# Padded strided cells, alternating value cells and a new issue plan in a banded-attention, SoLU and bilinear kernel

## Chip, cores and metric

One core of a Trainium2 chip. The metric is device microseconds of one execution; lower is better. Three runs of the kernel before gave 739.69, 740.57 and 744.24 us.

## What is computed

Three layers follow one another on 2304 tokens (4 batches of 576): causal attention with 8 heads of 64, then a SoLU layer with a layer norm, then a bilinear layer. In attention, heads 0 to 3 see the last 32 keys, and heads 4 to 7 see only the earlier keys whose position has the same remainder modulo 32.

```python
rel = pos[:, None] - pos[None, :]
mask_local = (rel >= 0) & (rel < stride)                                      # heads 0..3, stride 32
mask_strided = (rel >= 0) & (pos[None, :] % stride == pos[:, None] % stride)  # heads 4..7
attn = softmax(where(mask, q @ k.T / 8, -1e9)); x = attn @ v                  # (2304, 512)
h = x @ w_in; solu = h * softmax(h)                                           # w_in (512, 1024)
ln = (solu - mean) / sqrt(var + 1e-6) * g_ln; y = ln @ w_out                  # w_out (1024, 512)
return ((y @ w_a) * (y @ w_b)) @ w_out2                                       # d_ff = 1536
```

## The kernel before

All work is recorded first as a list of operations with an engine, an estimated duration, what they read and write, and a key. A planner (class `Plan`) then issues them: `forward` simulates the five engines, taking at each step the ready operation with the smallest key; `backward` sets new keys from a pass in reverse; 120 rounds with random noise on the keys (from `PARAM["seed"]`) are tried and the plan that its own replay finds shortest is kept. The duration passed to `pe(...)` is thus only a plan's cost, but it decides the order on every engine: TensorE, VectorE, ScalarE, GpSimd, and SyncE's queue of DMA issues. Engines run their instructions in the order issued and wait on semaphores.

**Attention.** Heads go in pairs ("groups"), four per batch: two strided, two local. `group_T` transposes q and k (L624) into `qkT`; for strided groups the evacuation (L632) sorts the positions by remainder, so that each of the 32 remainders is a run of 18 consecutive columns. A head's 16 runs of one parity (`RP`) are taken three at a time: 54 queries against the same 54 keys, a "cell", with the part between different runs masked off. Since 16 = 5 x 3 + 1, the sixth cell has one run: 18 queries and 18 keys (`RUNS`). `att_tile(g, j, ...)` handles one tile: a strided tile is two heads and one parity, 12 cells, two of them with 18 rows; a local tile is up to four blocks of 64 queries with 96 keys, for two heads, 8 cells. There are 16 strided and 24 local tiles in all, in four batches.

In a tile `scores` (L706, L709) writes the mask into a PSUM tile `s` with one full-size bf16 matmul per bank, then adds q k' of each cell. The cell's first operand is loaded as weights (its queries are the columns of the weight tile, 54 or 18 of them), its second moves (its keys). Upper and lower PSUM halves (`half`) alternate between cells; in a strided tile both heads read the partitions of one parity. fp32 operands take two passes, each with a record. Softmax follows on VectorE (maximum, subtraction, sum, reciprocal), ScalarE (exponential) and GpSimd (division, L784; in batch 0 L769 to L781 after it). The probabilities are transposed: in batch 0 in fp32 through TensorE (L769, "direct"), in the others as two fp16 parts by a DMA transpose (L793). `pv` multiplies with the values into `xbank`: in batch 0 one fp32 matmul per cell (L803), in the others three fp16 ones (L808 to L810). Here the values are the weight tile (keys are its rows, 64 value dimensions its columns), and the queries move. The rows of a strided cell start at partition 64 x head and the result lands at partition 64 x head. Then ScalarE writes the result to `xT` (L830).

**The layers behind.** `moe1` makes h with 24 matmuls per 128 tokens (L861), interleaved by the planner with attention; `s2` makes y (L910). Then comes the bilinear layer, matmuls M (L1288) and o (L1353), in three passes over w_a, w_b and w_out2, with fp16 weights split into two parts by ScalarE and VectorE (L1123 and others). Weights arrive in 64-bit form and are rebuilt by `from_f64` (L468 to L481). Of w_in and w_out this happens during the first 100 us.

The order of the cells in a strided tile and the plan's cost of the score operation:

```python
cells = [... for p in reversed(range(NG)) for h in range(2) for half in range(2)
         for r in (2 * p + half,) if r < len(RUNS) ...]
pe(ng * nk * 0.42e-3 + sum(0.04 if c[3] else 4 * c[7] / 2.4e3 for c in cells) + 0.03, scores, ...)
```

So the cells with the short run come second and fourth: head 0 with 54 rows, head 0 with 18, head 1 with 54, head 1 with 18, and then eight with 54.

Of the kernel before, what the change touches and what calls it, by code (L numbers as in the profile page):

```python
# [48 lines left out]
PSCALE = 4096.0  # L49
LSCALE = 1024.0  # L50
NEG = -(2.0 ** 120)
PASSES = ((0, 0), (0, 1), (1, 0))

PARAM = dict(back=12, first=40, early=(0,), seed=4, noise=0.1, direct=(0,), span=4.0, dense=1500, cols=5000, pf1=(),
             pf2=(), ph1=(), pv=(), pp=(8,), ps1=(), ps2=(), passes=120, e=3,
             PT=3, raw=2, rawl=2, raws=2, qkT=2, V=2, wk=2, xt=1, ln=2, lnT=2, ys=2, raw64=3, f64f=4, att=100.0,
             win=24.5, wout=128.6, moff=-69.7, moe=96.6, conv2=257.2, dconv=15.0, p2=385.0, pre=6.5, fine=(),
# [38 lines left out]
class Plan:  # L96
# [43 lines left out]
    def latency(self, a, b):  # L140
        if a.eng == b.eng and a.eng != "SP":
            return self.SAME[a.eng]
        return PARAM["lat"] * (0.28 if a.eng == "PE" else 0.14)

    def schedule(self):
# [4 lines left out]
        best, keys = self.length(order), [o.key for o in self.ops]  # L150
        rnd = random.Random(PARAM["seed"])
        for n in range(PARAM["passes"]):
            if n % PARAM["back"] == 0 and n >= PARAM["first"]:
                for o, key in zip(self.ops, keys):
# [4 lines left out]
            for o in self.ops:  # L159
                o.key += rnd.gauss(0.0, PARAM["noise"]) - o.sooner  # L160
            self.shift = self.TICK * (n % 4) / 4
# [73 lines left out]
    def forward(self):  # L235
# [13 lines left out]
        for _ in self.ops:  # L249
# [4 lines left out]
            if e == "PE":  # L254

                while recent and recent[0][0] < at - PARAM["span"]:
                    recent.popleft()
# [29 lines left out]
def tile_banded_attention_solu_bilinear(  # L287
# [13 lines left out]
    nc = tc.nc  # L301
# [5 lines left out]
    def pe(us, fn, r, w, cols=60): return P.op("PE", us, fn, r, w, cols)  # L307
# [107 lines left out]
    def keep(t, base, pattern, cm):  # L415
        nc.gpsimd.affine_select(out=t, in_=t, compare_op=ALU.is_ge, fill=NEG, base=base, pattern=pattern,
                                channel_multiplier=cm)
# [138 lines left out]
    groups = [[None] * (H // 2) for _ in range(B)]  # L556
    for b in range(B):
        for pr in range(H // 2):
            g = groups[b][pr] = Group()
# [111 lines left out]
    def att_tile(g, j, fine):  # L671
# [3 lines left out]
        direct = g.b in pm["direct"]  # L675
        i = counter[0]
        counter[0] += 1
        if g.strided:
            ng, nk, W, nx = 2 * NG, RC, 64, S // 2
            cells = [(h, j, (2 * p + h) * RC, half, r, n * NR, h * (S // 2) + a * NR, n * NR, h * (S // 2) + a * NR,  # L680
                      p, 64 * h, (r * 2 + j) * D)
                     for p in reversed(range(NG)) for h in range(2) for half in range(2)
                     for r in (2 * p + half,) if r < len(RUNS) for a, n in (RUNS[r],)]
        else:
            b0, nb = LT[j]
            nm = (nb + 1) // 2
            ng, nk, W, nx = 2 * nm, KB, 128, QB * nb
            cells = [(h, h, m * KB, half, b, QB, QB * b, KB, max(QB * b - ST, 0), h * nm + m, 0, (b * 2 + h) * D)
                     for m in range(nm) for half in range(2) for h in range(2)
                     for b in (b0 + 2 * m + half,) if b < b0 + nb]  # L690
# [9 lines left out]
        def scores():  # L700
            s = sp()
            last = {(c[1], c[3]): n for n, c in enumerate(cells)}
            for f in banks:
                for rows, stop in ([(slice(0, 128), False)] if len(last) == 2 * len(banks) else
                                   [(slice(64 * x, 64 * x + 64), (f, x) not in last) for x in range(2)]):
                    nc.tensor.matmul(s[rows, f, :npb * nk], identb[:, rows], mask[:, :npb], start=True, stop=stop)  # L706
            for n, (h, f, col, half, _, nq, q0, kk, k0, *_) in enumerate(cells):
                w = slice(64 * f, 64 * f + 64)
                nc.tensor.matmul(s[64 * half:64 * half + nq, f, col:col + kk], g.T()[w, 0, q0:q0 + nq],  # L709
                                 g.T()[w, 1, k0:k0 + kk], start=False, stop=n == last[f, half])  # L710
        pe(ng * nk * 0.42e-3 + sum(0.04 if c[3] else 4 * c[7] / 2.4e3 for c in cells) + 0.03, scores,
           ((g.T, 0), (g.T, 1), "identb", "masks" if g.strided else "maskl"), (sp,),
           ng * nk + sum(c[7] for c in cells))
        mx, e = rings["mx"].new(), rings["e"].new()
# [29 lines left out]
        PT = rings["PT"].new()  # L744
        if direct:
            early = g.b in pm["early"]
# [24 lines left out]
            def ptf():  # L771
                return blocks(PT().bitcast(F32).rearrange("p a n -> p (a n)"))
# [10 lines left out]
        else:  # L783
# [6 lines left out]
            else:  # L790
# [2 lines left out]
            dma(lambda: nc.sync.dma_start_transpose(out=PT()[:, :nblk], in_=P2[pi][:, :nblk * 128]),  # L793
                (("P2", pi, 0), ("P2", pi, 1)), (PT,), 28000 * nblk, us=0.2 + 0.125 * nblk)
        x = rings["x"].new()

        def pv():
            xf = x()
            for h, f, _, half, rb, nq, q0, kk, _, blk, p0, vc in cells:
                o0 = q0 - (h * (S // 2) if g.strided else QB * b0)  # L800
                o = xf[64 * h:64 * h + 64, o0:o0 + nq]
                if direct:
                    nc.tensor.matmul(o, g.rawv()[p0:p0 + kk, vc:vc + D], ptf()[p0:p0 + kk, blk, 64 * half:64 * half + nq],  # L803
                                     start=True, stop=True)
                    continue
                pt = [PT()[p0:p0 + kk, blk + hl * nblk // 2, 64 * half:64 * half + nq] for hl in range(2)]
                V = [V_()[p0:p0 + kk, vc:vc + D] for V_ in g.V]
                nc.tensor.matmul(o, V[0], pt[0], start=True, stop=False)  # L808
                nc.tensor.matmul(o, V[0], pt[1], start=False, stop=False)  # L809
                nc.tensor.matmul(o, V[1], pt[0], start=False, stop=True)  # L810
        if direct:
            pe(0.06 + sum(0.045 if c[0] else 4 * c[5] / 2.4e3 for c in cells), pv, (PT, *g.vtoks), (x,),
               sum(2 * c[5] * c[7] / 128 for c in cells))
        else:
            pe(0.06 + sum(0.07 if c[0] else 3 * c[5] / 2.4e3 + 0.01 for c in cells), pv, (PT, *g.V), (x,),
               sum(3 * c[5] * c[7] / 128 for c in cells))
        t0 = g.b * S % XR
        if g.strided:
# [19 lines left out]
    def moe1(t):  # L838
# [18 lines left out]
        for n in range(2):  # L857
            for pi, (xa, wa) in enumerate(PASSES):
                def mm(n=n, pi=pi, xa=xa, wa=wa):
                    for kk in range(4):  # L860
                        nc.tensor.matmul(h()[:, 512 * n:512 * n + 512], xs[xa]()[:, kk],  # L861
                                         win[wa][:, kk, 512 * n:512 * n + 512],
                                         start=(pi == 0 and kk == 0), stop=(pi == 2 and kk == 3))
# [39 lines left out]
    def s2(lnT, p, mh):  # L903
        y, ys = rings["y"].new(), rings["ys"].new()
        for mi in range(2):
            m = 2 * mh + mi
            for pi, (xa, wa) in enumerate(PASSES):
                def mm(mi=mi, m=m, pi=pi, xa=xa, wa=wa):
                    for kk in range(8):
                        nc.tensor.matmul(y()[:, 256 * mi:256 * mi + 256], wout[:, kk, wa, 128 * m:128 * m + 128], lnT()[:, xa, kk],  # L910
                                         start=(pi == 0 and kk == 0), stop=(pi == 2 and kk == 7))
# [53 lines left out]
    def attention(b):  # L965
        P.sooner = pm["sooner"]
        gs = order[4 * b:4 * b + 4]
        ts = batch_tiles(b)
        P.key = pm["att"] * b - pm["pre"]
        for p in (gs[:2], gs[2:]):  # L970
            for g in p:
                load_v(g)
            if b not in pm["direct"]:
                pair_scale(p)
        for n, (g, j) in enumerate(ts):
            P.key = pm["att"] * (b + n / len(ts))
            if not j:
                P.key -= pm["pre"]
                group_T(g)
                if b not in pm["direct"]:  # L980
                    group_v(g)
                load_next()
                P.key += pm["pre"]
            att_tile(g, j, (b * len(ts) + n) in pm["fine"])
        P.sooner = 0.0
# [293 lines left out]
    def product(y7, u, m):  # L1279
# [4 lines left out]
        def mult(bank, a, b, first):  # L1284
            def mm():
                for pi, (xa, wa) in enumerate(PASSES):
                    for kk in range(2):
                        nc.tensor.matmul(bank()[:, :HB], w()[:, wa, a, kk], y7[b]()[:, xa, kk],  # L1288
                                         start=first and pi == 0 and kk == 0, stop=pi == 2 and kk == 1,
                                         skip_group_check=not first)  # L1290
# [54 lines left out]
    def out_tile(ps, n, pus, tt, osc):  # L1345
# [3 lines left out]
        for u in range(UP):  # L1349
            def mm(u=u):  # L1350
                for c in range(2):
                    for pi, (xa, wa) in enumerate(PASSES):
                        nc.tensor.matmul(o(), pus[u]()[:, xa, c, 128 * tt:128 * tt + 128], wo()[:, 2 * u + c, wa],  # L1353
# [99 lines left out]
```

## Time and profile before

| | |
|---|---|
| three runs | 739.69, 740.57, 744.24 us (median 740.57) |
| profiled execution, first to last instruction | 742.1 us; what lies around it is not listed apart |
| TensorE busy (matmul) | 719.9 us, 97% |
| VectorE, ScalarE, GpSimd busy | 519.3, 432.2, 117.2 us |
| mean granted TensorE clock | 0.977 of 2.4 GHz |
| chain that ended last | TensorE 88%, VectorE 6%, ScalarE 2%, DMA 2% |

Matmuls are pipelined: a record's duration reaches from its start to its modelled end, and records of neighbours overlap. What a piece of work costs TensorE is therefore read from start to start, not from the durations. In the order of time, neighbours of one line are merged into a row with a count; a row asked for in a narrow stretch shows the first of the records that run there. The granted clock is 1.00 at 2.4 GHz and 0.50 at 1.2 GHz; the first change on record is at 43 us.

### The profile page before, as it was taken

To read this page: it belongs to the slowest core of one execution; us is meant where nothing else is said; L and a number is where in the kernel's file an instruction comes from. 1 tells how busy PE (TensorE), PEld (TensorE's weight loads), DVE (VectorE), ACT (ScalarE), POOL (GpSimd) and SP (SyncE) were. 2 spreads that over 40 slices of the span, in tenths; PEclk is the share of its full clock that TensorE was granted. 3 is DMA by queue.
4 is the path that set the end of the run, shared out by engine and by line. 5 is a ranking of instruction groups with operands and counts; after the bars stand their busy time and mean duration, and the time that the engine had idled before them with its cause. 6 is when DMAs were issued, how large, how long until landed. Compare 5 with 4: busy or idle time off the path is not lost.

```text
span 742.1 us, 14124 instructions
## 1 busy us (share of the span) xinstructions
PE 719.9 (97%) x5444; PEld 479.2 (65%) x5444; DVE 519.3 (70%) x1020; ACT 432.2 (58%) x824; POOL 117.2 (16%) x194
## 2 busy tenths in 40 slices
PE   6989889999999999999999999999999999999997
PEld 4867668888787888878655555555555546555553
DVE  4888987858776864898899998547868454434252
ACT  4667977676777876785768666544454333132230
POOL 4441435412433432210000000000000000000000
PEclk9988979999999999999999999999999999999999
DMA  9788996976998585567537034406705031711304
GB/s 212 181 193 222 193 153 136 221 178 160 218 208 165 118 190 141 149 123 254 194 142 272 20 129 129 142 28 187 246 1 170 29 126 44 236 57 46 124 6 165
DMA packets 159327, 109.61 MB, mean 148 GB/s; under 512 B 103702, under 2 KB 137500, under 8 KB 159260
## 3 DMA queue, kind: packets, MB, share of 16 engines
q1 hardware_dynamic: 159260, 108.71, 56.6%
q8 instruction: 43, 0.70, 0.4%
q14 instruction: 24, 0.20, 0.1%
HBM read 65.42 MB, written 27.53 MB: 125 GB/s over the span
## 4 chain that ended last, share of the span: by engine, by line
PE 88%; DVE 6%; ACT 2%; DMA 2%; issue 1%; SPq 0%; POOL 0%; POOLq 0%; DVEq 0%
PE M L1288 31%; PE o L1353 19%; PE y L910 12%; PE h L861 12%; PE s L709 4%; PE s L624 3%; PE xbank L808 2%; PE xbank L803 1%; PE s L706 1%; DMA raw<-in_moe_w_b_dram 1%; PE xbank L810 1%; DMA rawk<-in_k_dram 1%; DMA rawq<-in_q_dram 1%; PE xbank L809 1%; ACT qkT L632 1%
## 5 line engine op out<-in xcount | busy, mean ns | idle before, releaser
L1288 PE MATMUL M<-y,w 128*128 128x384 f16 x1512 | 256.4, 326 | 0.9 <-DVE y L1235 0.6
L1288 PEld LDWEIGHTS <-w 128*128 128x128 f16 x1512 | 147.8, 98 | 102.5 <-issue 1.6
L1353 PE MATMUL o<-wo,p 128*128 128x512 f16 x648 | 147.9, 379 | 0.0
L1353 PEld LDWEIGHTS <-p 128*128 128x128 f16 x648 | 63.3, 98 | 71.0
L910 PE MATMUL y<-lnT,wout 128*128 128x256 f16 x864 | 105.0, 279 | 0.8 <-ACT ys L913 0.6
L910 PEld LDWEIGHTS <-wout 128*128 128x128 f16 x864 | 83.9, 100 | 15.4 <-issue 2.5
L861 PE MATMUL h<-win,xh 128*128 128x512 f32 x288 | 81.5, 422 | 1.4 <-DVE wk L869 1.3
L1295 ACT COPY M<-M 128x384 f32<-128x384 f32 x72 | 33.5, 466 | 68.3 <-PE M L1288 68.2
L861 PEld LDWEIGHTS h<-win,xh 128*128 128x128 f32 x288 | 55.1, 201 | 13.2 <-DVE wk L869 1.1
L1338 ACT ACTIVATE p<-A 128x384 f16<-128x384 f32 x72 | 36.7, 520 | 33.2 <-DVE A L1337 33.1
L1360 DVE SCALAR_TENSOR_TENSOR ob<-o,osc,op 128x512 f32<-128x512 f32 x36 | 27.0, 750 | 40.4 <-PE o L1353 35.1
L1340 DVE SCALAR_TENSOR_TENSOR p<-A,p 128x384 f16<-128x384 f32 x72 | 38.8, 552 | 8.0 <-ACT p L1338 7.7
L709 PE MATMUL s<-qkT 64*54 64x54 f32 (+2 forms) x672 | 38.4, 254 | 2.7 <-ACT qkT L632 2.4
L1299 DVE TENSOR_TENSOR A<-M,V 128x384 f32<-128x384 f32 x36 | 20.0, 555 | 30.0 <-PE M L1288 29.9
L475 DVE SCALAR_TENSOR_TENSOR f64f<-f64f,raw 128x512 int32<-128x512 int32 x52 | 39.4, 762 | 1.4 <-ACT f64f L468 0.7
L866 DVE TENSOR_REDUCE st<-h 128x1 f32<-128x1024 f32 x18 | 22.0, 1221 | 25.9 <-PE h L861 25.9
L861 PE MATMUL h<-win,xl 128*128 128x512 f32 x144 | 40.0, 400 | 0.0
L1337 DVE TENSOR_TENSOR A<-A,M 128x384 f32<-128x384 f32 x36 | 19.9, 552 | 27.0 <-PE M L1288 26.8
L468 ACT ACTIVATE f64f<-raw 128x512 f32<-128x512 f32 x52 | 34.5, 670 | 7.1 <-DMA raw<-in_moe_w_out_dram 2.9
L1310 ACT COPY V<-M 128x384 f32<-128x384 f32 x36 | 17.1, 475 | 34.4 <-PE M L1288 34.3
L709 PEld LDWEIGHTS s<-qkT 64*54 64x54 f32 (+2 forms) x672 | 27.7, 143 | 13.4 <-issue 3.6
L784 POOL TENSOR_TENSOR e<-e,r 128x324 f32<-128x324 f32 (+2 forms) x30 | 26.6, 889 | 59.5 <-DVE r L740 59.5
(170 smaller groups left out, 1135.7 us busy)
## 6 DMA issues: line engine op xcount, KB each, us to landing
raw<-in_moe_w_out_dram SPq DMA_DIRECT2D x20, 512.0 KB
o_scr<-ob SPq DMA_DIRECT2D x36, 256.0 KB
op<-o_scr SPq DMA_DIRECT2D x36, 256.0 KB
raw<-in_moe_w_a_dram SPq DMA_DIRECT2D x12, 512.0 KB
raw<-in_moe_w_b_dram SPq DMA_DIRECT2D x12, 512.0 KB
y_scr<-y SPq DMA_DIRECT2D x14, 384.0 KB
y<-y_scr SPq DMA_DIRECT2D x14, 384.0 KB
y_scr<-ys SPq DMA_DIRECT2D x18, 256.0 KB
```

Of the source, the lines that this page charges most:

```text
L468: act(0.67, lambda: nc.scalar.activation(f(), raw()[:, :, 1].bitcast(F32), AF.Copy, scale=2.0 ** -112), (raw,), (f,))
L475: nc.vector.scalar_tensor_tensor(fi, fi, 3, raw()[:, :, 0], op0=ALU.logical_shift_left, op1=ALU.bitwise_or)
L709: nc.tensor.matmul(s[64 * half:64 * half + nq, f, col:col + kk], g.T()[w, 0, q0:q0 + nq], g.T()[w, 1, k0:k0 + kk], start=False, stop=n == ...
L784: pool(0.1 + 1.2 * pl, lambda: nc.gpsimd.tensor_tensor(ev(), ev(), r()[:, :ng].unsqueeze(2).to_broadcast([128, ng, nk]), op=ALU.mult), (r, ...
L861: nc.tensor.matmul(h()[:, 512 * n:512 * n + 512], xs[xa]()[:, kk], win[wa][:, kk, 512 * n:512 * n + 512], start=(pi == 0 and kk == 0), sto ...
L910: nc.tensor.matmul(y()[:, 256 * mi:256 * mi + 256], wout[:, kk, wa, 128 * m:128 * m + 128], lnT()[:, xa, kk], start=(pi == 0 and kk == 0), ...
L1288: nc.tensor.matmul(bank()[:, :HB], w()[:, wa, a, kk], y7[b]()[:, xa, kk], start=first and pi == 0 and kk == 0, stop=pi == 2 and kk == 1, s ...
L1295: act(TA, lambda: nc.scalar.copy(dst()[:, :HB], src()[:, :HB]), (src,), (dst,))
L1338: act(TA, lambda x=x, v=v: nc.scalar.activation(v(0), x(), AF.Copy, scale=2.0 ** -PEXP), (x,), ((pu, 0, c, t),))
L1340: dve(TD, lambda x=x, v=v: nc.vector.scalar_tensor_tensor(v(1), x(), 2.0 ** -PEXP, v(0), op0=ALU.mult, op1=ALU.subtract), (x, (pu, 0, c, t ...
L1353: nc.tensor.matmul(o(), pus[u]()[:, xa, c, 128 * tt:128 * tt + 128], wo()[:, 2 * u + c, wa], start=(u == 0 and c == 0 and pi == 0), stop=( ...
L1360: dve(0.75, lambda: nc.vector.scalar_tensor_tensor(ob(), o(), osc()[:, tt:tt + 1], op(), op0=ALU.mult, op1=ALU.add), (o, osc, op), (ob,))
```

## The change

Three things. In `scores`, the weight tile of a strided cell with 18 queries is read 36 columns wide (`LEAST`): 18 more columns of `qkT`, which lie behind it (for the last cell in the k part of the same tile, hence the flattened view). The 18 extra rows of the result land in rows of `s` that belong to no query. In `pv`, a strided cell takes 54 key rows always; for the short run the extra rows meet probabilities and values that are zero. Its cells are gone through with the heads in turn (`turns`): head 0, head 1, head 0, head 1; the local cells did so already. And the plan's costs of both operations are new: two changes of tile size per operation at `SWITCH` = 0.095 us, a price for each pair of cells, none for the second of a pair; the seed is 18 instead of 4.

```diff
+LEAST, SWITCH = 36, 0.095
...
-PARAM = dict(back=12, first=40, early=(0,), seed=4, noise=0.1, ...
+PARAM = dict(back=12, first=40, early=(0,), seed=18, noise=0.1, ...
...
+            qk = g.T().rearrange("p c s -> p (c s)")
             for n, (h, f, col, half, _, nq, q0, kk, k0, *_) in enumerate(cells):
-                w = slice(64 * f, 64 * f + 64)
-                nc.tensor.matmul(s[64 * half:64 * half + nq, f, col:col + kk], g.T()[w, 0, q0:q0 + nq],
+                w, nq = slice(64 * f, 64 * f + 64), max(nq, LEAST)
+                nc.tensor.matmul(s[64 * half:64 * half + nq, f, col:col + kk], qk[w, q0:q0 + nq],
                                  g.T()[w, 1, k0:k0 + kk], start=False, stop=n == last[f, half])
-        pe(ng * nk * 0.42e-3 + sum(0.04 if c[3] else 4 * c[7] / 2.4e3 for c in cells) + 0.03, scores,
+        groups = [c[7] for c in cells if not c[3] and (g.strided or not c[0])]
+        pe(ng * nk * 0.42e-3 + 2 * SWITCH + sum(4 * kk / 2.4e3 + 0.01 for kk in groups) + 0.03, scores,
...
+        turns = sorted(cells, key=lambda c: (-c[9], c[3], c[0])) if g.strided else cells
...
-            for h, f, _, half, rb, nq, q0, kk, _, blk, p0, vc in cells:
+            for h, f, _, half, rb, nq, q0, _, _, blk, p0, vc in turns:
+                kk = nk
...
-            pe(0.06 + sum(0.045 if c[0] else 4 * c[5] / 2.4e3 for c in cells), pv, (PT, *g.vtoks), (x,),
+            pe(2 * SWITCH + sum(4 * c[5] / 2.4e3 + 0.015 for c in cells if not c[0]), pv, (PT, *g.vtoks), (x,),
...
-            pe(0.06 + sum(0.07 if c[0] else 3 * c[5] / 2.4e3 + 0.01 for c in cells), pv, (PT, *g.V), (x,),
+            pe(2 * SWITCH + sum(3 * c[5] / 2.4e3 + 0.015 for c in cells if not c[0]), pv, (PT, *g.V), (x,),
```

TensorE, second score tile of the second strided group and what follows (`qkT` scores, `raws` values, `rawq` and `rawk` transposed inputs, `lnT` probabilities to be transposed); before:

```order
L709 MATMUL s<-qkT 18x18
L709 MATMUL s<-qkT 54x54 x8
L803 MATMUL xbank<-PT,raws_110 64x54
L803 MATMUL xbank<-PT,raws_110 64x18
L803 MATMUL xbank<-PT,raws_110 64x54
L803 MATMUL xbank<-PT,raws_110 64x18
L803 MATMUL xbank<-PT,raws_110 64x54 x8
L624 MATMUL s<-ident,rawq 128x96 x6
L624 MATMUL s<-ident,rawk 128x96 x6
L769 MATMUL y<-ident,lnT 128x128 x3
```

and now:

```order
L711 MATMUL s<-qkT 36x18
L711 MATMUL s<-qkT 54x54 x8
L772 MATMUL y<-ident,lnT 128x128 x3
L625 MATMUL s<-ident,rawq 128x96 x6
L808 MATMUL xbank<-PT,raws_110 64x54 x2
L808 MATMUL xbank<-PT,raws_110 64x18 x2
L808 MATMUL xbank<-PT,raws_110 64x54 x8
L625 MATMUL s<-ident,rawk 128x96 x6
L808 MATMUL xbank<-PT,raws_110 64x54 x2
L808 MATMUL xbank<-PT,raws_110 64x18 x2
L808 MATMUL xbank<-PT,raws_110 64x54 x8
```

The score cell has 36 rows, the two short value cells stand together, and the first two value tiles follow one another with only six transposes between them.

SyncE, the first DMA issues (`raws` are strided values, `raw` a piece of w_in); before:

```order
L574 DMA rawq<-in_q_dram 96x6x128
L574 DMA rawk<-in_k_dram 96x6x128
L591 DMA raws_110<-in_v_dram 18x6x128
L591 DMA raws_110<-in_v_dram 18x5x128
L580 DMA rawq<-in_q_dram 96x6x64 x2
```

and now:

```order
L575 DMA rawq<-in_q_dram 96x6x128
L575 DMA rawk<-in_k_dram 96x6x128
L464 DMA raw_177<-in_moe_w_in_dram 128x1024
L592 DMA raws_110<-in_v_dram 18x5x128
L592 DMA raws_110<-in_v_dram 18x6x128
```

A 512 KB piece of w_in goes ahead of the first values.

## Rows read from the trace of the kernel before

**Rows 1.** Stretches: length, busy us (count) PE, PEld, DVE, ACT, POOL, clock, DMA, GB/s.

```profile
8.47:43.15 34.68, 33.14 (x318) 27.09 (x318) 23.92 (x43) 19.79 (x40) 12.06 (x14) 1.00 0.90 211
43.15:125.00 81.85, 73.19 (x731) 55.98 (x730) 71.69 (x141) 65.84 (x129) 29.86 (x41) 0.83 0.82 174
125.00:300.00 175.00, 174.29 (x1834) 140.49 (x1832) 122.93 (x233) 127.01 (x240) 61.47 (x105) 0.98 0.81 175
330.00:742.10 412.10, 406.63 (x2341) 228.76 (x2339) 269.13 (x539) 189.84 (x377) 0.00 (x0) 1.00 0.39 126
63.63:70.46 6.83, 6.83 (x45) 5.57 (x45) 6.83 (x16) 4.89 (x11) 1.00 (x2) 0.50 0.95 239
```

**Rows 2.** Order of time, TensorE, a strided score tile: start us, us, engine, line, operation.

```profile
133.40 0.31 PE L706 MATMUL s<-masks,identb 128*128 128x324 bf16 x1
133.64 1.36 PE L709 MATMUL s<-qkT 64*54 64x54 f32 x24
...
133.87 0.40 PE L709 MATMUL s<-qkT 64*18 64x18 f32 x3
...
134.39 0.26 PE L709 MATMUL s<-qkT 64*54 64x54 f32 x2
...
134.53 0.37 PE L709 MATMUL s<-qkT 64*54 64x54 f32 x8
...
134.63 0.37 PE L709 MATMUL s<-qkT 64*54 64x54 f32 x8
...
134.93 0.31 PE L706 MATMUL s<-masks,identb 128*128 128x324 bf16 x1
```

**Rows 3.** Order of time, TensorE, a strided fp16 value tile.

```profile
100.61 0.21 PE L808 MATMUL xbank<-PT,V 54*64 54x54 f16 x1
...
100.81 0.19 PE L808 MATMUL xbank<-PT,V 18*64 18x18 f16 x1
...
101.39 0.21 PE L808 MATMUL xbank<-PT,V 54*64 54x54 f16 x1
...
101.48 0.21 PE L808 MATMUL xbank<-PT,V 54*64 54x54 f16 x2
...
101.97 0.34 PE L706 MATMUL s<-maskl,identb 128*128 128x192 bf16 x2
```

**Rows 4.** Order of time, TensorE, a local fp16 value tile.

```profile
119.85 0.23 PE L808 MATMUL xbank<-PT,V 96*64 96x64 f16 x2
...
119.96 0.21 PE L808 MATMUL xbank<-PT,V 96*64 96x64 f16 x2
...
120.35 0.27 PE L522 MATMUL xbank<-ident,am 128*2 128x128 f32 x1
```

**Rows 5.** Groups by line and shape: the short cells: count | busy us, mean ns.

```profile
L709 PE MATMUL s<-qkT 64*18 64x18 f32 x64 | 7.1, 187 | 0.0
...
L808 PE MATMUL xbank<-PT,V 18*64 18x18 f16 x24 | 4.7, 195 | 0.0
...
L803 PE MATMUL xbank<-PT,raws 18*64 18x18 f32 x16 | 3.2, 278 | 0.0
```

**Rows 6.** Order of time, TensorE, score and fp32 value tiles of batch 0.

```profile
8.47 2.04 PE L709 MATMUL s<-qkT 64*54 64x54 f32 x24 [0.84 <-ACT qkT L632]
...
9.52 0.34 PE L709 MATMUL s<-qkT 64*54 64x54 f32 x2
...
10.45 0.45 PE L706 MATMUL s<-masks,identb 128*128 128x324 bf16 x1
...
27.91 2.52 PE L803 MATMUL xbank<-PT,raws 54*64 54x54 f32 x24
30.36 0.90 PE L769 MATMUL y<-ident,lnT 128*128 128x128 f32 x3
...
42.10 1.12 PE L803 MATMUL xbank<-PT,rawl 96*64 96x64 f32 x16
43.15 0.34 PE L706 MATMUL s<-maskl,identb 128*128 128x192 bf16 x2
```

More of the change, by code (lines that the diff above doesn't have):

```diff
@@ L51 @@
 NEG = -(2.0 ** 120)
+LEAST, SWITCH = 36, 0.095
 PASSES = ((0, 0), (0, 1), (1, 0))
-PARAM = dict(back=12, first=40, early=(0,), seed=4, noise=0.1, direct=(0,), span=4.0, dense=1500, cols=5000, pf1=(),
+PARAM = dict(back=12, first=40, early=(0,), seed=18, noise=0.1, direct=(0,), span=4.0, dense=1500, cols=5000, pf1=(),
              pf2=(), ph1=(), pv=(), pp=(8,), ps1=(), ps2=(), passes=120, e=3,
```

## Prediction

> **What bounds the kernel now.** I read first the stretches of the span [rows 1]. From 125 to 300 us TensorE is busy 174.29 of 175 us while VectorE has 122.93 and ScalarE 127.01; from 330 us to the end it is busy 406.63 of 412.10. In both it sets the pace. Before that it does so only in part: from 8.47 to 43.15 us it is busy 33.14 of 34.68 (VectorE 23.92), and from 43.15 to 125 us it has 73.19 and VectorE 71.69 of 81.85, so that there neither is free. The change touches attention alone, which ends near 300 us; the last 412 us hold the same matmuls as before.
>
> "Busy" does not say that the array does useful work, so I read next the order in time inside one attention tile, at full clock. A strided score tile takes 133.64 to 134.93, 1.29 us [rows 2]. The reader is to see the starts: the first cell starts at 133.64, the 18-row cell behind it at 133.87, and the first cell of the next group only at 134.39. Four cells (54, 18, 54, 18 rows) took 0.75 us one after the other; the eight cells of 54 rows that follow take 0.54, drain included, and start two by two: 134.39, 134.53, 134.63. The cells with 18 rows are thus the dear ones, though they move a third of the columns: at each change between a weight tile of 18 columns and one of 54 nothing overlaps.
>
> The value tiles show the same [rows 3]: 100.61 to 101.39 for the first four cells (0.78 us; here the tile changes in its rows, 54 keys against 18), and 101.39 to 101.97 for the other eight. There only one of two neighbours overlaps, since the order is head 0, head 0, head 1, head 1: the row at 101.39 is a single, that at 101.48 a pair. The local value tile alternates its heads already [rows 4]: eight cells, wider ones (64 queries, 96 keys), take 119.85 to 120.35, 0.50 us, in pairs every 0.11.
>
> **The change, part by part.**
>
> *18 rows padded to 36 (scores).* No instruction more or less: twelve cells per tile stay, and the order still reads 54, 18, 54, 18 columns, but the weight tile has 36 columns in place of 18. If 36 goes with 54, the first four cells are two more pairs; the trace has weight tiles of 18, 54, 64 and 128 columns and none of 36, so its price lies between that of the pairs and that of today's four single cells (nothing saved). I take the pairs. The Trainium skill, "TensorEngine Tiling (Array Packing)", Tiling Modes, knows parts of 32, 64 or 128 columns, by which 36 belongs with 54; no run here shows it yet. At full clock a pair costs 0.10 (134.53 to 134.63 [rows 2]), so the tile takes 0.54 + 2 x 0.10 = 0.74 instead of 1.29: 0.55 saved. The dearest that the rows allow is a quarter of the 0.54 with its start and drain, 0.135 a pair: 0.48 saved. Sixteen strided tiles (64 records of 18 columns, two passes of two cells each [rows 5]): four before 43.15 us, four up to 125, eight from 125 to 300. The first four run at half clock: the same 24 records take 2.04 us there and 1.36 at 133.64 [rows 2, 6]; the granted clock of that stretch reads 1.00, but no change of it is on record there, and I go by the durations. Their first four cells take 1.05 (8.47 to 9.52), the rest 0.93. Priced at 0.93/4 = 0.23 a pair they save 1.05 - 0.46 = 0.59 each.
>
> *54 keys in every value cell, heads in turn.* The added keys meet zeros; the moving width stays. Twelve cells in six pairs, by the local tile: 0.50 + 2 x 0.11 = 0.72 against 1.36, 0.64 saved. This tile does not stand in the trace. From below: if heads did not pair at all, twelve single slots of 0.09 (101.39 to 101.48) with the closing 0.1 make 1.18, 0.18 saved; from above, pairs of 18 queries could cost nothing, 0.75. I take 0.64, nearest the local tile, which has the same alternation. Twelve such tiles (24 records [rows 5]): four before 125 us, eight behind. The four fp32 tiles of batch 0 take 27.91 to 30.36 = 2.45 at half clock; the local fp32 tile of eight cells takes 42.10 to 43.15 = 1.05 [rows 6], so twelve cost at most 1.05 x 12/8 = 1.58: 0.87 saved.
>
> Sum of TensorE time: up to 43.15 us 4 x 0.59 + 4 x 0.87 = 5.8; up to 125 us 4 x 0.55 + 4 x 0.64 = 4.8; up to 300 us 8 x 0.55 + 8 x 0.64 = 9.5. Together 20.1 us.
>
> *What of it reaches the end.* From 125 to 300 us the others have some 50 us free, so I count nine tenths, 8.6; what is late next is the softmax chain of VectorE, ScalarE and GpSimd, whose latency a shorter TensorE queue covers less well. From 43.15 to 125 us VectorE is as full as TensorE: between 0 and 4.8, I take half, 2.4. Before 43.15 us TensorE carries the chain, but what follows is the VectorE work on w_in and w_out: between 0 and 5.8, half, 2.9. Sum 13.9.
>
> *The order.* Both the costs and the seed are new, so every engine's order differs in attention: at the start two fp32 value tiles stand together now instead of either side of transposes, and SyncE issues one 512 KB piece of w_in ahead of the first values. At the 211 GB/s of [rows 1] that piece keeps the values back by 2.5 us, but their first matmul comes behind a score tile and a softmax, so I cost it at nothing; without that cover it is 2.5 us once. The new costs stand nearer the trace: a strided non-fp32 value tile was planned at 0.90 us and took 1.36, and is now planned at 0.64 where I expect 0.72; a local score tile was planned near 1 us. A truer plan should help, a redrawn one may hurt. The bounds: waits in the stretch 43.15 to 125 (81.85 - 73.19 = 8.7 us) could go, or as many could come. I take 0 and keep 6 each way, two thirds of the bound.
>
> Against the profiled span: 742.1 - 13.9 = 728.2, with what lies around it unchanged. The runs' median, 740.57, stands 1.5 below that span, so the forecast in the runs' terms is 726.7 us, 1.9% faster. About 1%, 7.4 us, is what a measurement of this kernel can tell from no change.
>
> **The rivals.**
>
> *The gain becomes waits.* Up to 125 us VectorE sets the pace and returns nothing; from 125 to 300 us, where a tile's softmax must be ready sooner, half comes back: 4.8 us, 735.8. For it: VectorE at 71.69 of 81.85. Against: 174.29 of 175 behind it.
>
> *All of it arrives and the plan gains.* TensorE is on the chain almost throughout: 20.1 us, and a little from shorter waits: 719. For it: 33.14 of 34.68 even at the start.
>
> *One half does nothing.* Alternating heads use other partitions of the operands but one PSUM bank. If they don't overlap, each fast value tile saves 0.18 instead of 0.64 and the fp32 ones nothing: 20.1 - 12 x 0.46 - 3.5 = 11.1, of which 13.9/20.1 arrives, 7.7: 732.9. If it is 36 columns that stay a size of their own, the scores' 4 x 0.59 + 12 x 0.55 = 9.0 are missing: 11.1 again and the same time. Against the first: the local tile pairs heads in the same bank at 0.11 a pair [rows 4]. The Trainium skill states its rule in "TensorEngine Tiling (Array Packing)", Gotcha 1: PSUM Pressure (different row tiles cannot use one bank at once); by [rows 4] it does not bind where the column halves differ too.
>
> *Slower.* A TensorE with less to do waits for softmax results, and its clock falls to half: in 63.63 to 70.46 us it was granted 0.50 with TensorE busy 6.83 us throughout [rows 1], 3.4 us lost. In the stretch 43.15 to 125 the clock is 0.83 already. This decides from four such stretches more than before (13.9/3.4); at six and a half the kernel is 1% slower, 748 and up, say 750. Against: from 125 to 300 us the clock is 0.98 and dense work (the matmuls of h and y) is always ready between tiles.
>
> **How the numbers follow.** The forecast (726.7, own range 720 to 733) has 0.59; all of it and more (719) 0.15; waits (735.8) 0.16; one half idle (732.9) 0.06; slower (750) 0.04. The slower case and a part of the waits are left out of the range: 715 (719 less a share of the 6 of the order) to 737. Faster by over 1%, below 733.2: the forecast less a tail of 0.01, the 0.15, half of the idle half and 0.04 of the waits, 0.80. Slower by over 1%: 0.04. The rest, 0.16, is within 1%.
>
> **What would show it.** A strided score tile in the fast stretch taking some 0.74 us to the next mask matmul, its cells in six pairs; a strided value tile taking 0.72; the mean of TensorE's 36-column records no different from the others. Attention ending some 14 us earlier, the stretch behind it as long as before. It is wrong if TensorE's idle time up to 300 us grows by more than 6 us, if cells of 36 rows still stand alone, or if the granted clock between 43 and 125 us falls well under 0.83.

## The result and the profile after

The changed kernel takes 721.09 us (median; 720.25 to 722.64) against 740.17 (739.69 to 744.24): a ratio of 0.9738, 95% interval 0.971 to 0.9766, 19.1 us less. The forecast was 726.7 with 715 to 737, faster. Each execution's time is about 2.1 us more than its profiled span: the profile after has a span of 720.5 us in an execution of 722.64, so the profile before (742.1) belongs to the run of 744.24.

TensorE in order of time, a strided score tile at full clock, from its mask to what follows; columns as in [rows 2]:

```profile
116.70 0.30 PE L707 MATMUL s<-masks,identb 128*128 128x324 bf16 x1
116.93 0.80 PE L711 MATMUL s<-qkT 64*54 64x54 f32 x24
117.66 0.23 PE L813 MATMUL xbank<-PT,V 96*64 96x64 f16 x2
```

From 116.93 to 117.66 are 0.73 us, where [rows 2] had 1.29 from start to start. A strided fp16 value tile, and one of the fp32 ones of batch 0 with the transposes behind it, answering to [rows 3] and [rows 6]:

```profile
149.90 0.22 PE L813 MATMUL xbank<-PT,V 54*64 54x54 f16 x2
...
150.01 0.18 PE L813 MATMUL xbank<-PT,V 54*64 54x18 f16 x2
...
150.11 0.20 PE L813 MATMUL xbank<-PT,V 54*64 54x54 f16 x2
...
150.59 0.28 PE L915 MATMUL y<-lnT,wout 128*128 128x256 f16 x1
...
21.10 1.53 PE L808 MATMUL xbank<-PT,raws 54*64 54x54 f32 x24
22.57 1.22 PE L625 MATMUL s<-ident,rawk 96*128 96x96 f32 x6
```

The reader is to see that every row of the fp16 tile counts two, the short cells with their 18 queries as well: six pairs every 0.10, 149.90 to 150.59 = 0.69 us (1.36 before). The fp32 tile takes 1.47 us at half clock (21.10 to 22.57; 2.45 before). The same 5444 matmuls keep TensorE busy 695.0 us instead of 719.9:

```profile
PE 695.0 (96%) x5444; PEld 460.3 (64%) x5444; DVE 518.0 (72%) x1020; ACT 432.5 (60%) x824; POOL 126.3 (18%) x194
```

The stretches that answer to [rows 1] (same columns):

```profile
8.47:43.15 34.68, 30.58 (x379) 24.75 (x380) 29.36 (x60) 24.18 (x54) 17.07 (x16) 0.91 1.04 232
43.15:125.00 81.85, 73.17 (x790) 56.87 (x789) 75.31 (x145) 69.03 (x135) 34.72 (x45) 0.87 0.97 190
125.00:300.00 175.00, 173.36 (x1861) 141.23 (x1860) 132.40 (x252) 138.56 (x250) 63.98 (x105) 1.00 0.84 183
```

At the start TensorE now has room (30.58 of 34.68) and VectorE works more in the same time (29.36 against 23.92). Behind 125 us TensorE is still full, and VectorE and ScalarE stay below 140 of 175.

### The profile page after: what moved, and what is told of

It reads as the page before. It is cut to its first block, busy times and chain, and to the rows that moved or that the text cites. A ratio compares the mean times of both kernels' runs of the same rounds, so it can differ in the third digit from the quotient of the medians.

```text
span 720.5 us, 14110 instructions
## 1 busy us (share of the span) xinstructions
PE 695.0 (96%) x5444; PEld 460.3 (64%) x5444; DVE 518.0 (72%) x1020; ACT 432.5 (60%) x824; POOL 126.3 (18%) x194
## 4 chain that ended last, share of the span: by engine, by line
PE 81%; DVE 8%; DMA 4%; ACT 3%; issue 2%; SPq 1%; POOL 1%; DVEq 0%; ACTq 0%; POOLq 0%
PE M L1293 33%; PE o L1358 19%; PE y L915 11%; PE h L866 10%; PE s L711 3%; DMA raw<-in_moe_w_out_dram 2%; DVE f64f L476 1%; PE s L625 1%; DMA raw<-in_moe_w_b_dram 1%; PE xbank L813 1%; PE s L707 1%; DMA rawk<-in_k_dram 1%; ACT qkT L633 1%; DVE f64f L482 1%; DVE e L734 1%
## 5 line engine op out<-in xcount | busy, mean ns | idle before, releaser
L915 PE MATMUL y<-lnT,wout 128*128 128x256 f16 x864 | 102.1, 276 | 2.2 <-ACT ys L918 1.3
L866 PE MATMUL h<-win,xh 128*128 128x512 f32 x288 | 79.8, 419 | 1.2 <-DVE wk L874 1.2
L1304 DVE TENSOR_TENSOR A<-M,V 128x384 f32<-128x384 f32 x36 | 19.9, 556 | 38.9 <-PE M L1293 38.9
L469 ACT ACTIVATE f64f<-raw 128x512 f32<-128x512 f32 x52 | 34.7, 673 | 13.9 <-DMA raw<-in_moe_w_out_dram 5.0
L1342 DVE TENSOR_TENSOR A<-A,M 128x384 f32<-128x384 f32 x36 | 19.9, 553 | 30.9 <-PE M L1293 29.8
L787 POOL TENSOR_TENSOR e<-e,r 128x324 f32<-128x324 f32 (+2 forms) x30 | 28.3, 947 | 43.7 <-DVE r L743 42.5
L795 POOL TENSOR_TENSOR P<-e,P 128x324 f16<-128x324 f32 (+2 forms) x30 | 31.2, 1043 | 19.0 <-ACT P L794 19.0
L711 PE MATMUL s<-qkT 64*54 64x54 f32 (+2 forms) x672 | 28.6, 248 | 4.5 <-ACT qkT L633 3.9
```

The lines of the kernel that those rows point to most:

```text
L469: act(0.67, lambda: nc.scalar.activation(f(), raw()[:, :, 1].bitcast(F32), AF.Copy, scale=2.0 ** -112), (raw,), (f,))
L787: pool(0.1 + 1.2 * pl, lambda: nc.gpsimd.tensor_tensor(ev(), ev(), r()[:, :ng].unsqueeze(2).to_broadcast([128, ng, nk]), op=ALU.mult), (r, ...
L795: pool(0.15 + 1.4 * pl, lambda: nc.gpsimd.tensor_tensor(plo, ev(), ph, op=ALU.subtract), (e, ("P2", pi, 0)), (("P2", pi, 1),))
```

## The experiments

Three theories stood against each other. A: the 20 us of TensorE time all reach the end, the order is worth nothing. B, that of the prediction with one term mended: about two thirds arrive, and the new order adds the rest. C: the order is the larger part. "Old order" means the issue order of the kernel before, "new order" that of the changed kernel.

**The new cells in the old order.** Against the changed kernel: the old costs (that of the fp32 value operation likewise) and seed 4, so that every engine issues as before; the changes of `scores` and `pv` stay.

```diff
-PARAM = dict(back=12, first=40, early=(0,), seed=18, noise=0.1, ...
+PARAM = dict(back=12, first=40, early=(0,), seed=4, noise=0.1, ...
...
-        pe(ng * nk * 0.42e-3 + 2 * SWITCH + sum(4 * kk / 2.4e3 + 0.01 for kk in groups) + 0.03, scores,
+        pe(ng * nk * 0.42e-3 + sum(0.04 if c[3] else 4 * c[7] / 2.4e3 for c in cells) + 0.03, scores,
...
-            pe(2 * SWITCH + sum(3 * c[5] / 2.4e3 + 0.015 for c in cells if not c[0]), pv, (PT, *g.V), (x,),
+            pe(0.06 + sum(0.07 if c[0] else 3 * c[5] / 2.4e3 + 0.01 for c in cells), pv, (PT, *g.V), (x,),
```

> Padded score cells and alternating 54-key value cells in the issue order of the kernel before (old costs, old seed). Theory A (cells alone: nearly all of the some 20 us of TensorE time reaches the end): 719 to 723 us, score tile 0.73 and value tile 0.69 us at full clock. Theory B (two thirds of it arrives, as predicted, and the new plan adds the remaining 5 to 6 us): 725 to 728. Theory C (the plan is the larger part): above 730.

Measured: 727.2 us, ratio 0.9818 (0.9791 to 0.9845), 13.2 us less than the 740.4 of its own comparison. That is theory B.

**The new order with the old cells.**

```diff
...
-                w, nq = slice(64 * f, 64 * f + 64), max(nq, LEAST)
+                w = slice(64 * f, 64 * f + 64)
...
-            for h, f, _, half, rb, nq, q0, _, _, blk, p0, vc in turns:
-                kk = nk
+            for h, f, _, half, rb, nq, q0, kk, _, blk, p0, vc in cells:
...
```

> The new issue order (new costs, seed 18) with the old cells: strided score tiles 1.29 us and value tiles 1.36 us again. Theory A: the order alone is worth nothing, 738 to 743 us. Theory B: it is worth 5 to 6 us, 734 to 736. Theory C: more than 8 us, below 732. A fourth outcome, the new order made for short tiles is worse with long ones: above 744.

Measured: 737.1 us, ratio 0.9952 (0.9931 to 0.9972), 3.3 us less. This lies between A and B: the order helps the old cells too. It adds 727.2 - 721.1 = 6.1 us to the new ones; that this is more is not clear of the noise, for the intervals reach 1.5 to 2 us each way.

**One half at a time, old order.** The scores alone:

```diff
-                w = slice(64 * f, 64 * f + 64)
+                w, nq = slice(64 * f, 64 * f + 64), max(nq, LEAST)
...
```

> Only the score cells padded to 36 rows, everything else as before, old issue order. TensorE time saved by the rows: 4 x 0.6 to 0.7 and 12 x 0.55, about 9 us. Theory A: 730 to 732 us. Theory B (two thirds): 733 to 735. Theory C: above 737.

Measured: 730.1 us, ratio 0.9866 (0.9832 to 0.99), 10.3 us less: theory A for this half. The values alone (`turns` as in the change):

```diff
-            for h, f, _, half, rb, nq, q0, kk, _, blk, p0, vc in cells:
+            for h, f, _, half, rb, nq, q0, _, _, blk, p0, vc in turns:
+                kk = nk
```

> Only the value cells changed (54 keys always, heads in turn), old issue order. TensorE time saved: 12 x 0.67 and 4 x 0.98, about 12 us. Theory A: 727 to 730 us. Theory B (two thirds): 731 to 734. Theory C: above 737.

Measured: 732.66 us, ratio 0.9892 (0.9857 to 0.9928), 7.7 us less: theory B. The halves make 18.0 us one by one and 13.2 together; by the spans of the profiles below it is 20.4 and 16.1. So they do not add. Where they fail to, the second profile of before and the start times below show.

**Before, once more.**

> The kernel before once more, for a second profile: 738 to 744 us. The first profile came from a run of 744.24 us and shows two stretches at half clock behind 125 us (166 and 231 us). If those are what makes that run longer than the median, a run near 740 lacks one or both; if not, they are there again.

Measured: 740.95 us, span 738.7, 3.4 less than in the first profile. In the first, two stretches behind 125 us were at half clock:

```profile
166.03:169.45 3.42, 3.42 (x13) 2.82 (x12) 3.15 (x11) 2.18 (x5) 0.15 (x1) 0.50 0.46 141
230.89:234.30 3.41, 3.41 (x18) 2.43 (x17) 3.41 (x7) 0.69 (x2) 1.54 (x3) 0.50 0.61 187
```

In the second there is none:

```profile
125.00:300.00 175.00, 173.71 (x1845) 140.65 (x1844) 124.88 (x240) 129.87 (x243) 62.52 (x104) 1.00 0.82 176
```

Half of 6.8 us is 3.4 us. Of the difference 0.6 us is there at the first matmul of h already (51.23 against 50.66), and 2.7 come between the fifth h and the last values, where the two stretches lie. So the second profile is the one to compare stages with. Starts in us, read from each profile's order of time (the first matmul of h for the first and for the fifth 128 tokens, and the last value matmul of attention):

```
                          h, 1st   h, 5th   last values   span    median
before, second profile     50.7    126.7      295.9       738.7   740.2 to 740.6
scores alone, old order    47.1    120.1      283.7       726.5   730.1
values alone, old order    48.7    123.3      287.7       730.5   732.7
both, old order            47.6    120.0      279.8       722.6   727.2
old cells, new order       47.7    124.9      292.2       735.1   737.1
changed kernel             43.4    118.2      277.7       720.5   721.1
```

(The profile of "both, old order" is of its fastest execution, 724.79 us.) Up to the fifth h the scores alone bring 6.6 us, the values alone 3.4, both together 6.7. From there to the last values they bring 5.6, 4.8 and 9.4. So the halves nearly add behind 120 us and do not before it. From the last values to the end all six kernels take 442.8 or 442.9 us: every difference arises before them, as the prediction had it. The scores alone bring more (10.3 us, 12.2 by span) than the 9.4 us of TensorE time that they save; with them the granted clock first rises at 24.8 us and not at 42.9, but that this is the reason was not tried.

**What holds the first 50 us.** The chain that ended last, cut to 20 to 48 us, by line; before (first profile), and the new cells in the old order:

```profile
by line: PE xbank L803 33.3%; PE s L709 15.8%; PE s L624 14.4%; PE y L769 11.9%; DVE raw L470 5.5%; DVE e L731 5.3%; PE s L706 4.8%; DVE mx L722 4.7%; DVE f64f L475 2.5%; DVE f64f L481 2.1%; issue 2.1%; DVE sm L735 1.7%; DVE r L740 0.7%; DV
```

```profile
by line: DVE f64f L476 25.7%; DVE f64f L482 23.2%; DVE raw L471 15.2%; DVE e L733 9.2%; DVE sm L737 6.5%; DVE mx L724 6.1%; issue 5.4%; ACT e L736 3.2%; ACT f64f L469 2.1%; DVE r L742 2.0%; ACT win L497 1.8%; ACT PT L783 1.7%; ACT sm L741 0
```

Four TensorE lines led it; with the new cells the rebuild of the weights on VectorE does (the three lines of `f64f` and `raw`). A chain is an inference, so it was tried: the last two steps of the rebuild of w_in on 32 of 512 columns, in both kernels, with the order unchanged (n = 32 for w_in, and the same in the step for the sign). This leaves out the low bits and signs of w_in's other columns.

```diff
-            fi = f().bitcast(I32)
-            nc.vector.scalar_tensor_tensor(fi, fi, 3, raw()[:, :, 0], op0=ALU.logical_shift_left, op1=ALU.bitwise_or)
+            fi = f().bitcast(I32)[:, :n]
+            nc.vector.scalar_tensor_tensor(fi, fi, 3, raw()[:, :n, 0], op0=ALU.logical_shift_left, op1=ALU.bitwise_or)
...
```

> The new cells in the old order (727.2 us) with the last two VectorE steps of the rebuild of w_in done on 32 of 512 columns: it leaves out most of the low bits and signs of w_in and takes some 9 us of VectorE work out of the first 50 us, with the same instructions in the same order. If VectorE's rebuild bounds the first 50 us once the cells are short, the first h matmul comes 3 us or more earlier than 47.6 us and the time falls to 720 to 724. If TensorE or the DMA still bounds that stretch, 726 to 728.

Measured: ratio 0.9786 (0.9728 to 0.9844); the runs went from 721.45 to 729.36, with one of 2422 us, so the median says little. It was repeated:

> The new cells in the old order with the lighter rebuild of w_in once more, in more rounds, since the first answer spread from 721 to 729 us. If the early VectorE work carries through to the end, 721 to 725 us against 727.2 of the same cells without the cut, that is some 3 us or more against the 1.6 that the cut brought the kernel before; if it is given back behind the first h matmul, 726 to 728.

Measured: 723.78 us (719.12 to 727.74), ratio 0.9774 (0.974 to 0.9808): 3.4 us less than the same cells without the cut, though the two intervals overlap. The first h matmul starts at 42.5 and 42.8 us in the two profiles, against 47.6. In the kernel before:

> The kernel before with the same cut in the rebuild of w_in (same part left out). If TensorE bounds the first 43 us with the old cells, it gains clearly less than the new cells do: 0 to 2 us, 738 to 741. If VectorE bounds it there too, 3 us or more as with the new cells: 737 or less.

Measured: 739.04 us, ratio 0.9978 (0.9961 to 0.9994), 1.6 us less; first h at 49.35 against 50.66 us. So the same 9 us or so of VectorE work move the first h by 1.3 us with the old cells and by 5 with the new ones: for the first 50 us the chain was right that the bound changes hands. How much of the 5 lasts to the end is less sure; TensorE then waits 4.9 us once behind 51 us for a `qkT` of ScalarE (1.6 without the cut). At the fifth h 2.6 and 1.2 us of it are left (117.4 and 118.8 against 120.0), while the old cells have 3.2 there (123.4 against 126.7, with 6.8 us less at half clock between the first rise and 125 us). So between 50 and 125 us the test does not tell which engine holds the time.

**Which widths count alike.**

```diff
-LEAST, SWITCH = 36, 0.095
+LEAST, SWITCH = 32, 0.095
```

> The changed kernel with strided cells of 18 rows read 32 columns wide instead of 36, same order of issue. If what counts is a class of tile size whose boundary lies between 32 and 36 (54 on the other side), the strided score tile goes back to 1.29 us at full clock, some 9 us of TensorE time come back and the time is 727 to 731 us. If any equal-looking width or the mere padding helped, 720 to 723 us with tiles of 0.73.

Measured: 728.54 us, ratio 0.9835 (0.9792 to 0.9879), 7.4 us more than with 36. A strided score tile of it, and the groups of its score cells by shape:

```profile
118.03 1.39 PE L711 MATMUL s<-qkT 64*54 64x54 f32 x24
119.35 0.23 PE L813 MATMUL xbank<-PT,V 96*64 96x64 f16 x2
```

```profile
L711 PE MATMUL s<-qkT 64*54 64x54 f32 x320 | 22.5, 244 | 2.8 <-ACT qkT L633 2.5 <-ACT sm L742 0.2
...
L711 PE MATMUL s<-qkT 64*32 64x18 f32 x64 | 8.0, 202 | 0.0
```

and with 36:

```profile
L711 PE MATMUL s<-qkT 64*54 64x54 f32 x320 | 15.6, 239 | 4.1 <-ACT qkT L633 3.9 <-ACT sm L742 0.2
...
L711 PE MATMUL s<-qkT 64*36 64x18 f32 x64 | 5.5, 201 | 0.0
```

The tile takes 1.32 us, near the 1.29 of before. The means hardly differ (202 and 201 ns, 244 and 239), so the mean, which the prediction named as a sign, tells nothing; the busy time differs (8.0 and 5.5 us, 22.5 and 15.6), since with 36 the records overlap. Padding as such brings nothing; going beyond a boundary between 32 and 36 columns does.

**Keys without turns.**

```diff
-            for h, f, _, half, rb, nq, q0, kk, _, blk, p0, vc in cells:
+            for h, f, _, half, rb, nq, q0, _, _, blk, p0, vc in cells:
+                kk = nk
```

> Of the value cells only the 54 keys, the heads in the old order (two of one head, then two of the other), old plan. If the change of tile size is all that matters, the fp16 strided value tile takes the same 0.69 us as with both. If the pairing of heads matters too, twelve cells in that order take seven slots in place of six: 0.75 to 0.80 us. If alternation is most of it, above 1.0.

Measured: 731.53 us in a single execution. The tile:

```profile
111.03 0.21 PE L809 MATMUL xbank<-PT,V 54*64 54x54 f16 x1
...
111.12 0.21 PE L809 MATMUL xbank<-PT,V 54*64 54x54 f16 x2
...
111.62 0.19 PE L809 MATMUL xbank<-PT,V 54*64 54x54 f16 x1
...
111.80 0.28 PE L911 MATMUL y<-lnT,wout 128*128 128x256 f16 x1
```

The tile takes 0.77 us in seven slots: a single cell, five pairs, a single cell. Of the 0.67 us saved in a value tile the keys bring 0.59, and the turns on top of them 0.08. The turns without the keys were not run.

**Costs or seed.** The changed kernel with the old seed, then the new cells with the old costs and the new seed.

```diff
-PARAM = dict(back=12, first=40, early=(0,), seed=18, noise=0.1, ...
+PARAM = dict(back=12, first=40, early=(0,), seed=4, noise=0.1, ...
```

> The changed kernel with seed 4 instead of 18: new cells, new costs, another draw of the plan. If the truer costs bring the 6 us by which the changed kernel beats the same cells in the old order (727.2), 720 to 723 us. If it is the draw, 725 to 730.

Measured: 730.49 us, ratio 0.9858 (0.9805 to 0.9911).

```diff
-        pe(ng * nk * 0.42e-3 + 2 * SWITCH + sum(4 * kk / 2.4e3 + 0.01 for kk in groups) + 0.03, scores,
+        pe(ng * nk * 0.42e-3 + sum(0.04 if c[3] else 4 * c[7] / 2.4e3 for c in cells) + 0.03, scores,
...
-            pe(2 * SWITCH + sum(3 * c[5] / 2.4e3 + 0.015 for c in cells if not c[0]), pv, (PT, *g.V), (x,),
+            pe(0.06 + sum(0.07 if c[0] else 3 * c[5] / 2.4e3 + 0.01 for c in cells), pv, (PT, *g.V), (x,),
```

> New cells, old costs, seed 18. If the seed brings the 6 us, 720 to 723 us; if the costs do, 725 to 730.

Measured: 732.7 us, ratio 0.9893 (0.985 to 0.9935). So neither the costs nor the seed carries the 6 us. With the same cells, four draws of the plan gave 721.1, 727.2, 730.5 and 732.7 us. The draws differ in how long TensorE waits, and about half of what the two poorer ones add lies behind 125 us. In the order of before with the new cells, then the new costs with seed 4, then the old costs with seed 18:

```profile
125.00:300.00 175.00, 173.36 (x1915) 141.11 (x1914) 134.66 (x260) 138.77 (x256) 60.64 (x108) 1.00 0.85 188
125.00:300.00 175.00, 170.51 (x1886) 138.76 (x1885) 131.83 (x257) 136.57 (x254) 62.19 (x108) 0.99 0.91 187
125.00:300.00 175.00, 170.75 (x1898) 138.50 (x1897) 128.87 (x253) 135.82 (x252) 62.06 (x107) 1.00 0.85 180
```

TensorE is idle for 1.6, 4.5 and 4.3 us here (1.6 in the changed kernel), and for 9.4, 11.4 and 13.2 us from 43.15 to 125 us (8.7). The cells are worth 13 us in the order of before and 16 in the new one (737.1 - 721.1), a difference within the intervals; the new order is the best draw of four, and how its seed was chosen is not on record.

## Why the prediction was right, and where a term was off

*The cells.* Right, a little low: score tile 0.74 expected, 0.73 measured; value tile 0.72, and 0.69; fp32 value tile at most 1.58, and 1.47; score tile at half clock 1.39, and 1.29 (8.34 to 9.63):

```profile
8.34 1.36 PE L711 MATMUL s<-qkT 64*54 64x54 f32 x24 [0.80 <-ACT qkT L633]
9.63 0.45 PE L707 MATMUL s<-masks,identb 128*128 128x324 bf16 x1
```

With these the sum of TensorE time is 4 x 0.68 + 4 x 0.98 + 12 x 0.56 + 12 x 0.67 = 21.4 instead of 20.1; TensorE's busy time fell by 22.0, from 717.0 in the second profile of before to 695.0. The rival in which one half does nothing is refuted on both sides: 36 columns go with 54, and the heads pair, six matmuls in 0.10 us, though both write one PSUM bank (`xbank`). The Trainium skill, "TensorEngine Tiling (Array Packing)", Gotcha 1: PSUM Pressure, has the rule that different row tiles cannot use one bank at once. It does not bind for these cells: every row of the value tile at 149.90 counts two. The local tile of [rows 4], which the prediction names for this, is no case of it: its cells all lie on partitions 0 to 95, and its two heads differ in the column half alone. The pair at 101.48 in [rows 3] was the row to go by; there the rows differ as well.

*What reaches the end.* 13.9 us were expected in the old order, and 13.2 measured in it. By stage, in the profiles of both, the share was 8.6 us behind 125 us, and 9.4 came behind the fifth h; 5.3 before it, and 6.7 came. These make 16.1, since the profile is of an execution 2.4 us faster than the median; so the nearness of 13.9 and 13.2 is in part luck, the more as both halves before 125 us were taken midway between nothing and all. That TensorE's gain is cut because VectorE's rebuild of w_in comes next is shown by the lighter rebuild for the first 50 us; from there to 125 us, and for w_out, it is argued. TensorE's idle time up to 300 us grew from 16.6 us (16.1 in the second profile) to 19.9, less than the 6 us more that were named as a sign of being wrong. What was not seen is that, in these profiles, the scores alone bring all of it before the fifth h: 6.6 of the 6.7 us.

*The order.* Here is the term that was off: "I take 0 and keep 6 each way". The order was worth 6.1 us on the new cells, just past the bound, and 3.3 on the old ones, and it makes the distance between the forecast and the result (5.6 us). The bound had the right size, for the four draws lie up to 6 us on either side of 727.2, but in part by luck: it was worked out from TensorE's waits between 43.15 and 125 us, and about half of the waits that the two poorer draws add lies behind 125 us, where it counted none. What an order that differs everywhere is worth could not be read from the rows; the sentence that "a truer plan should help" is not borne out, since the same costs with another seed gave 730.5. One thing that this draw does better stood in the SyncE rows of the change: its first h matmul starts at 43.4 us and not at 47.6, with a piece of w_in ahead of the first values. That piece was costed at nothing for its delay of the values, and its gain (w_in is rebuilt sooner, just where VectorE's rebuild sets the pace) was not weighed. That it alone makes the 4 us was not tried, and at the fifth h only 1.8 of them are left (118.2 against 120.0), 2.1 in the span. These two profiles are of the slowest execution of the one kernel and the fastest of the other, so where the 6.1 us of the medians arise stays open.

*The slower rival.* The half clock behind 43.15 us came to 34.1 us in the first profile of before, 27.3 in its second one, and 20.8 after; from 43.15 to 125 us the granted clock was 0.87 against 0.83. So it did not come. But the clock rose for the first time at 29.8 us rather than at 43, and fell again at 36.6 us, where TensorE had begun to wait (busy 1.52 of the 3.62 us from 33.00 on); counted from that first rise the half clock is 27.3 us after, too.

## What to carry to other kernels

Read small matmuls from start to start: a matmul that is small and stands next to larger ones can cost more than they do, and rows whose counts stay at one where neighbours count two show it. Pad the odd one to the size class of the others and order them so that neighbours use different partitions, as the two heads do here. Where a planner redraws the whole order, give its draw a term of its own width, several us here, and compare changes in one fixed order before crediting them.

## What the runs showed that was not expected

A few columns decide what a strided cell costs: 32 leave the tile at 1.32 us, 36 bring 0.73. Two executions of one kernel differ by 2.7 us over two short stretches at half clock. And the new cells let the clock rise sooner but not stay: in the old order, where nothing else differs, it was full from 25.9 us (43 before) and at half again from 29.3 to 49.8 us, after TensorE had been busy 1.70 of 3.44 us,

```profile
29.31:49.80 20.49, 17.42 (x176) 13.27 (x175) 18.94 (x34) 14.31 (x32) 9.60 (x8) 0.50 0.95 212
```

with VectorE busy 18.94 of 20.49 us there, and leading the chain above: that stretch belongs to VectorE.
